# The first product of a mixture layer in seven block products instead of eight, with weight sums made on the chip

## The chip, the cores and the metric

The kernel runs on 1 core of one Trainium2 chip. The metric is the device time of one execution in microseconds, the median over the runs; before the change it is 940.54 us (3 runs, 940.5 to 940.66).

## The reference

Attention over a window of 128 keys with a bias that falls with distance, and behind it two matrix products with a squared Relu between them:

```python
def _attn_ref(q, k, v):                     # each (8, 8, 576, 64)
    scores = scale * np.matmul(q, k.transpose(0, 1, 3, 2))
    ...
    mask = (rel >= 0) & (rel < window)      # window = 128
    scores = np.where(mask, scores + bias[None], -1000000000.0)
    ...
    attn = attn / (np.sum(attn, axis=-1, keepdims=True) + 1e-09)
    return np.matmul(attn, v)

def _moe_ref(x, w_in, w_out):               # (4608, 512), (512, 2048), (2048, 512)
    h = np.maximum(x @ w_in, 0.0)
    return h * h @ w_out
```

x is the attention's output with the heads put side by side. All is float32.

## The kernel before

The 4608 tokens are cut into 9 chunks c of 512, and the 2048 hidden columns into 16 blocks f of 128. Everything is kept transposed: features on the partitions, tokens on the columns. Each float32 operand of the two large products is split into a high and a low part (type float32r), and a product is the sum of three: high by high, high by low, low by high.

**First product** (`gemm1`, L192; matmuls L200): for one chunk and one block f, four slices of 128 input features by three parts, 12 matmuls of 128x128 weights and 512 columns, into one bank `g` of the accumulation memory. Then a Relu on ScalarE (ACT, L210), the square on VectorE (DVE, L213), the high part on ACT (L217) and the low part on DVE (L219). **Second product** (`gemm2`, L221; matmuls L229): 12 matmuls more, four output blocks m by three parts, into four banks `acc` that collect over the 16 blocks f.

**Weights.** All 16 slots of an arena in the on-chip memory hold one block f of both matrices each (`weights_load`, L160). They come in as 64 bit floats and are converted on the chip (`convert`, L167) to a high and a low word that lie side by side, so the columns of a weight block are 8 bytes apart. In some blocks (`APART`, L39: first matrix, every fourth f, first two slices) neighbouring columns are dealt to two blocks, which makes the step 16 bytes. The weights stay on the chip to the end.

**Attention.** A `Couple` q is a pair of heads of a chunk; four make one chunk's x. A `visit` (L533) does, on the PE, the products of the old couple with its values (L541), in two phases, and between them the scores of the new couple (L548), which go into a pair of banks `big` (the same that `g` uses, one buffer) and into `s`. Then ACT and DVE take the scores out (`front`), `out` (L524) makes the x parts of the old couple (ACT high, DVE low), and `soft` and `squares` make the weights of the new couple: minimum on DVE, exponential on ACT (L257), normalisation on POOL (L269), a transpose on DVE (L321), four DMAs to DRAM (L325), one DMA back (L330), and two masks on POOL (L334). The second half of a couple is done in `rest`, whose exponentials are ordered behind the Relu of a first product. The next visit needs both halves.

**Order.** PE's order is written out by hand; the other engines are put in order by the compiler's scheduler, by priority and by its own estimate of time; blocks under `high_priority` go first. Chunk 0 and the first couples run under a planner (`Plan`, L632) with costs and due times in `start` (L683). From block n = 16 on a loop (L807) does the first product of block n and the second product of block n - 2 in turn, and every fourth n (`FIRST` = 39, counted in half steps) a visit between the two. All DMAs but a few go through the queue of SyncE (SP).

The accumulation memory is full: `s` two banks, `acc` four, `big` two.

Of the kernel before, what the change touches and what calls it, by code (L numbers as in the profile page):

```python
# [12 lines left out]
I32 = mybir.dt.int32  # L13
# [14 lines left out]
HEAT = 16  # L28
HOLD = lambda f: (('n', 3),) if f < 1 else (('n', 6),) if f < 2 else (('z', 7),)
# [8 lines left out]
FIRST = 39  # L38
# [23 lines left out]
class Kern:  # L62
    def __init__(self, ctx, tc, qkd, vd, w1d, w2d, cstd, outd):
        self.tc, self.nc = tc, tc.nc
        self.qkd, self.vd = qkd, vd
        self.w1d, self.w2d, self.cstd, self.outd = w1d, w2d, cstd, outd
# [9 lines left out]
        self.dr = ep("dr", 4, space=bass.MemoryType.DRAM)  # L76
        self.sc = ep("sc", 1, space=PSUM)
# [16 lines left out]
        self.start_banks = [self.ac.tile([128, 512], F32, name="acc") for _ in range(4)]  # L94

    def join(self, ctx):
        self.later.close()
        self.big = ctx.enter_context(self.tc.tile_pool(name="big", bufs=1, space=PSUM))
# [61 lines left out]
    def weights_load(self, f):  # L160
        nc = self.nc
        at = lambda name, dt: nc.alloc_sbuf_tensor_at(f"{name}{f}", [128, 2, 512, 2], dt, offset=self.arena + f * 8192).ap()
        self.raw[f], self.w[f] = at("raw", I32), at("w", F32R)
        for i, d in enumerate((self.w1d, self.w2d)):
            nc.sync.dma_start(self.raw[f][:, i].rearrange("p d t -> p (d t)"), d[f].bitcast(I32))
# [17 lines left out]
    def block(self, i, f, b):  # L183

        w = self.w[f][:, i]
# [34 lines left out]

    def gemm2(self, c, f):  # L221
        nc = self.nc
# [3 lines left out]
        for m in range(4):  # L226
# [5 lines left out]
            if f == NF - 1:  # L232
# [3 lines left out]
                (nc.scalar if c == NCH - 1 and m == 3 else nc.sync).dma_start(out, o)  # L236

# [135 lines left out]
class Couple:  # L373
# [150 lines left out]
    def out(self, S):  # L524
# [4 lines left out]
        self.K.nc.scalar.copy(halves(self.u[:, 0]), self.X)  # L529
        self.nc.vector.tensor_tensor(halves(self.u[:, 1]), self.X, halves(self.u[:, 0].bitcast(F32)), op=ALU.subtract)  # L530


def visit(K, old, new):  # L533
# [18 lines left out]
    for made in phase((1, 0), False)[:2]:  # L552
        K.tc.add_manual_dep(made.ins, turn.ins.name, SYNC, reason="halves of the keys change banks")
    if new:
        new.front()
    old.out(S)
# [126 lines left out]
def start(K):  # L683
# [91 lines left out]
    for f in range(NF + 2):  # L775
        if f < NF:
            g = K.gemm1(0, f)
            step, n = lambda g=g: next(g, None), len(CONVERT) - 1
            if f == 0:
                P.add("g1a", "PE", 2.1, tuple(last) + (("c", f, n),), GO, step, "g")  # L780
                last = ["g1a", ("l", 6), ("l", 7)]
            P.add(("g1", f), "PE", 2.8 if f else 0.7, tuple(last) + (("c", f, n),), 500 if f else GO, step, "g" if f else None)
# [6 lines left out]
        if 1 < f < NF:  # L789
            P.add(("g2", f - 2), "PE", 2.8, (("g1", f), ("h1", f - 2, 3)), 500, do(K.gemm2, 0, f - 2))  # L790
# [5 lines left out]
def tile_attn_moe(ctx: ExitStack, tc: tile.TileContext, *aps):  # L796
    K = Kern(ctx, tc, *aps)
    K.const()
    with tc.manual_schedule(engines={ENGINES["PE"]}):
# [7 lines left out]
        for n in range(NF, NF * NCH + 2):  # L807
            for t in (2 * n, 2 * n + 1):
                q, part = divmod(t - FIRST, 8)
                q += 9  # L810
                with tc.high_priority(offset=50):
                    if part == 0:
                        if q + 1 < 4 * NCH:
                            K.load(*divmod(q + 1, 4))
                        if q < 4 * NCH:
                            late = pairs[q] = Couple(K, q)
                        if q - 1 in pairs:
                            visit(K, pairs.pop(q - 1), late)
                        if late:
                            late.turn(0)  # L820
                if t % 2 == 0 and n < NF * NCH:
                    for _ in K.gemm1(*divmod(n, NF)):
                        pass
                    if late:
                        with tc.high_priority(offset=50):
                            late.rest()
                            late.turn(1)
                        late = None
                if t % 2:
                    K.gemm2(*divmod(n - 2, NF))  # L830
# [57 lines left out]
```

## Time and profile before

| | us |
|---|---|
| median of 3 runs | 940.54 |
| the profiled execution | 940.21 |
| its span | 938.5 |
| chunk 0 (36.8 to 137.7) | 100.9 |
| one chunk after it (137.7 to 238) | 100.3 |
| TensorE matmuls busy | 928.9 |
| VectorE, ScalarE, GpSimd busy | 501.5, 417.4, 210.2 |

The profile is of one execution. PE is TensorE's matmuls, PEld its weight loads, which run beside matmuls; DVE is VectorE, ACT ScalarE, POOL GpSimd, SP SyncE. A row of a group names line, engine, operation, out<-in, shapes and count, then busy time in us and the mean of one in ns, then the idle time of the engine before them and what ended it. A row of a timeline has the start in us, the length in us, the instructions and their count. Matmuls overlap in the pipeline, so the distance from start to start counts and not the recorded length.

### The profile page before, as it was taken

To read this page: it belongs to the slowest core of one execution; us is meant where nothing else is said; L and a number is where in the kernel's file an instruction comes from. 1 tells how busy PE (TensorE), PEld (TensorE's weight loads), DVE (VectorE), ACT (ScalarE), POOL (GpSimd) and SP (SyncE) were. 2 spreads that over 40 slices of the span, in tenths; PEclk is the share of its full clock that TensorE was granted. 3 is DMA by queue.
4 is the path that set the end of the run, shared out by engine and by line. 5 is a ranking of instruction groups with operands and counts; after the bars stand their busy time and mean duration, and the time that the engine had idled before them with its cause. 6 is when DMAs were issued, how large, how long until landed. Compare 5 with 4: busy or idle time off the path is not lost.

```text
span 938.5 us, 19487 instructions
## 1 busy us (share of the span) xinstructions
PE 928.9 (99%) x7488; PEld 782.9 (83%) x7492; DVE 501.5 (53%) x1334; ACT 417.4 (44%) x1107; POOL 210.2 (22%) x254
## 2 busy tenths in 40 slices
PE   8899999999999999999999999999999999999998
PEld 5688888888888888888888888888888888888886
DVE  6999874445554555545555454555455455433222
ACT  7898753343444444334434343334444444322222
POOL 4213331222221222222222222221222222220000
PEclk9999999999999999999999999999999999999999
DMA  9975424222433333232433232324322231111001
GB/s 341 404 287 167 136 73 130 72 62 82 130 86 85 83 99 108 63 86 80 124 85 86 77 105 77 86 85 121 94 76 83 75 92 43 38 46 45 1 0 45
DMA packets 72894, 95.26 MB, mean 101 GB/s; under 512 B 8033, under 2 KB 41953, under 8 KB 72801
## 3 DMA queue, kind: packets, MB, share of 16 engines
q1 hardware_dynamic: 72368, 93.36, 32.6%
q8 instruction: 59, 0.97, 0.4%
q10 hardware_dynamic: 432, 0.66, 0.3%
q14 instruction: 35, 0.28, 0.1%
HBM read 67.76 MB, written 26.21 MB: 100 GB/s over the span
## 4 chain that ended last, share of the span: by engine, by line
PE 95%; DMA 3%; DVE 1%; ACT 1%; issue 0%; POOLq 0%; DVEq 0%
PE acc L229 43%; PE g L200 42%; PE s L541 5%; PE g L548 2%; DMA raw<-in_dram 2%; PE s L548 1%; PE at L346 1%; DMA wide<-in_dram 1%; DMA qk<-in_dram 0%; ACT t L470 0%; PE s L412 0%; PE at L412 0%; DVE t L482 0%; DVE pp L625 0%; DVE tw L609 0%
## 5 line engine op out<-in xcount | busy, mean ns | idle before, releaser
L200 PE MATMUL g<-xu,w 128*128 128x512 f32 x1728 | 423.5, 394 | 1.4 <-issue 0.8
L200 PEld LDWEIGHTS g<-xu,w 128*128 128x128 f32 x1728 | 344.4, 209 | 56.8 <-issue 1.7
L229 PE MATMUL acc<-hh,w 128*128 128x512 f32 x1152 | 385.8, 396 | 0.0
L229 PEld LDWEIGHTS acc<-hh,w 128*128 128x128 f32 x1152 | 224.0, 194 | 45.7 <-issue 5.3
L210 ACT ACTIVATE r<-g 128x512 f32<-128x512 f32 x144 | 86.2, 599 | 352.4 <-PE g L200 352.2
L213 DVE TENSOR_TENSOR r<-r 128x512 f32<-128x512 f32 x129 | 92.4, 716 | 254.0 <-ACT r L210 254.0
L229 PE MATMUL acc<-hl,w 128*128 128x512 f32 x576 | 226.5, 393 | 0.0
L219 DVE TENSOR_TENSOR hl<-r,hh 128x512 fp32r<-128x512 f32 x144 | 122.0, 847 | 74.9 <-ACT hh L217 72.8
L334 POOL TENSOR_SCALAR_AFFINE_SELECT pp<-pp 128x512 f32<-128x512 f32 x128 | 109.8, 858 | 221.4 <-DMA pp<-way 173.5
L269 POOL TENSOR_TENSOR t<-t,nm 128x512 f32<-128x512 f32 x64 | 74.9, 1172 | 260.6 <-DVE nm L265 233.5
L229 PEld LDWEIGHTS acc<-hl,w 128*128 128x128 f32 x576 | 112.2, 195 | 19.6
L217 ACT CAST hh<-r 128x512 fp32r<-128x512 f32 x144 | 89.3, 620 | 78.2 <-DVE r L213 76.7
L257 ACT ACTIVATE t<-t,nm 128x128 f32<-128x128 f32 x256 | 100.1, 394 | 11.3 <-DVE nm L250 11.2
L321 DVE STREAM_TRANSPOSE pp<-t 128x512 f32<-128x512 f32 x64 | 45.1, 707 | 44.3 <-POOL t L269 38.6
L250 DVE CUSTOM_DVE_ANT_0 t<-t,cst 128x128 f32<-128x128 f32 x256 | 59.0, 295 | 1.0
L541 PE MATMUL s<-pp,v 64*64 64x128 f32 (+1 forms) x1792 | 52.0, 248 | 0.1
L541 PEld LDWEIGHTS s<-pp,v 64*64 64x64 f32 x1792 | 40.5, 134 | 10.1 <-issue 9.7
L257 ACT ACTIVATION_READ_ACCUMULATOR t<-t,nm 128x1 f32 x256 | 48.7, 190 | 0.0
L482 DVE COPY_PREDICATED t<-cst,s 64x256 f32<-64x256 int32 x100 | 44.5, 445 | 6.9 <-ACT t L463 3.8
L472 POOL MEMSET t<- 64x128 f32 (+1 forms) x44 | 10.0, 229 | 117.2 <-PE s L548 110.1
L529 ACT CAST xu<-s 128x512 fp32r<-128x512 f32 x28 | 16.4, 587 | 41.8 <-DVE t L482 26.9
L470 ACT COPY t<-g 64x256 f32<-64x256 f32 (+2 forms) x86 | 27.9, 340 | 3.7 <-PE g L548 1.0
(68 smaller groups left out, 480.5 us busy)
## 6 DMA issues: line engine op xcount, KB each, us to landing
raw<-in_dram SPq DMA_DIRECT2D x32, 512.0 KB, 8.7
way<-pp SPq DMA_DIRECT2D x256, 64.0 KB, 2.0
pp<-way SPq DMA_DIRECT2D x64, 256.0 KB, 2.7
qk<-in_dram SPq DMA_DIRECT2D x32, 320.0 KB, 3.1
v<-in_dram SPq DMA_DIRECT2D x32, 320.0 KB, 3.9
qk<-in_dram SPq DMA_DIRECT2D x38, 256.0 KB, 4.3
out_dram<-o SPq DMA_DIRECT2D x35, 256.0 KB, 2.6
v<-in_dram SPq DMA_DIRECT2D x3, 256.0 KB, 5.3
```

Of the source, the lines that this page charges most:

```text
L200: nc.tensor.matmul(g, w, xs[cc][:, part], start=i == 0, stop=i == 11)
L210: self.relu = nc.scalar.activation(r, g, AF.Relu)
L213: nc.vector.tensor_tensor(r, r, r, op=ALU.mult)
L217: nc.scalar.copy(hh, r)
L219: nc.vector.tensor_tensor(hl, r, hh.bitcast(F32), op=ALU.subtract)
L229: nc.tensor.matmul(self.acc[m], w, h, start=(f == 0 and i == 0), stop=(f == NF - 1 and i == 2))
L250: self.nc.vector.tensor_tensor_reduce(self.t[:, m], self.t[:, m], self.K.nrel(2 * self.p + m // 2), -0.125, BIG, ALU.add, ALU.min, self.nm ...
L257: return self.nc.scalar.activation(self.t[:, m], self.t[:, m], AF.Exp, bias=nm[:, 4 + m : 5 + m], scale=-1.0, accum_out=nm[:, m : m + 1],)
L269: self.nc.gpsimd.tensor_tensor(*(x.rearrange("p (j i) c -> p j i c", j=2) for x in (self.t, self.t)), self.rec.unsqueeze(3).to_broadcast([ ...
L321: nc.vector.transpose(squares.rearrange("p b m c -> p m b c"), self.t.rearrange("p m (b c) -> p m b c", c=32))
L334: nc.gpsimd.affine_select(to, self.own, pattern=[[-32 * sign, 4], [0, 4], [-sign, 32]], compare_op=op, fill=0.0, base=0, channel_multiplie ...
L541: made.append(mm(to, w, x, start=first and n < 2, stop=not first, skip_group_check=True))
```

## The change

In chunks 0 and 1 the first product stays as it was. From chunk 2 on (7 chunks) it is made for two blocks f at once (`seven`): the 512 input features, the 256 hidden columns and the 512 tokens are each halved, and the 2x2 block product is made of seven block products after Strassen and Winograd instead of eight. Each is 2 slices by 3 parts, 6 matmuls of 128x128 weights and 256 columns. The products are collected in two banks, which take the place of `big`: P in one, on which four products are summed one after the other, R and Q in the other. After each product ACT copies or DVE copies or adds the bank to a tile `four` of the on-chip memory; then Relu and square are one DVE instruction, and high and low part follow as before. Between the products stand the quarters of a second product (`second`), and a whole second product behind them.

Four of the seven weight operands are sums of weight blocks. `weight_sums` makes them once, in chunk 1, two pairs of blocks at each of the four visits there: seven operations on POOL, one on ACT, one on DVE, DMAs of all seven operands to DRAM (1.835 MB for a pair of blocks). `stream` brings the seven operands of a pair back in two DMAs into one of two buffers `flow`, for each of the 56 pairs. The buffers lie in the arena, in slots of first-matrix weights that are done with; for that the arena's 16 units now hold two blocks f of one matrix each (`UNITS`), loaded in the order in which they are first needed.

The four x operands that are sums are made in `out`: `tee` for the first two couples of a chunk (ACT 3, DVE 2, POOL 1 instructions of 256 columns in place of ACT 1 and DVE 1 of 512), `tees` for the last two (three more subtractions on DVE, three more copies on ACT, three subtractions on POOL). For the last couple of a chunk `out` goes ahead of `front`. `rest` now comes behind the first of the seven products, its exponentials behind the copy of P.

The diff, cut to its core:

```diff
+UNITS = [(0, 0)] + [x for p in range(NF // 2 - 1) for x in ((0, p + 1), (1, p))] + [(1, NF // 2 - 1)]
+UNIT = lambda i, f: UNITS.index((i, f // 2))
-FIRST = 39
+FIRST = 19
...
+    def weight_sums(self, j):
+        nc, sums = self.nc, self.sums[j]
...
+        for k, x in ((0, one), (3, words(w, 0)[:, 1]), (5, words(w, 1)[:, 1])):
+            nc.sync.dma_start(sums[:, k], x)
+        for m in range(2):
+            nc.gpsimd.tensor_tensor(lo[:, m], w[:, m, :, 0], w[:, m, :, 1], op=ALU.add)
...
+        nc.gpsimd.tensor_tensor(s1, a21, a22, op=ALU.add)
+        nc.gpsimd.tensor_tensor(as11(s2), as11(s1), a11, op=ALU.subtract)
+        nc.gpsimd.tensor_tensor(as11(s3), a11, as11(a21), op=ALU.subtract)
+        nc.gpsimd.tensor_tensor(s4, a12, s2, op=ALU.subtract)
+        nc.scalar.copy(lo.bitcast(F32R), hi)
+        nc.vector.tensor_tensor(hi.bitcast(F32R), hi, lo, op=ALU.subtract)
+        nc.sync.dma_start(sums[:, 1:3], words(both, 1))
+        nc.sync.dma_start(sums[:, 4:7:2], words(both, 0))
+
+    def stream(self, n):
+        if n >= NCH * NF // 2:
+            return
+        sums = self.sums[n % 8]
+        for i, x in enumerate(self.flow[n % 2]):
+            self.nc.sync.dma_start(x.bitcast(F32), sums[:, 4 * i : 4 * i + 4 - i])
...
+    def seven(self, n):
+        nc = self.nc
+        c, j = divmod(n, 8)
+        one, two = self.banks("one", "two")
+        P = one.tile([128, 512], F32, name="chain")[:, 0:256]
+        g = two.tile([128, 512], F32, name="rest")
+        R, Q = g[:, 0:256], g[:, 256:512]
+        four = self.four
+        def product(to, i, name, start=False):
+            todo = []
+            for (wh, wl), (xh, xl) in zip(self.operand(n, i), self.halves(c, name)):
+                todo += [(wh, xh), (wl, xh), (wh, xl)]
+            for k, (w, x) in enumerate(todo):
+                nc.tensor.matmul(to, w, x, start=start and k == 0, stop=k == 5, skip_group_check=True)
+        first = lambda: self.tc.high_priority(offset=600)
+        add = lambda to, x: nc.vector.tensor_tensor(to, to, x, op=ALU.add)
+        product(P, 0, "B11", True)
+        with first():
+            self.relu = nc.scalar.copy(four[:, 0, 0:256], P)
+        yield
+        product(R, 1, "T1", True)
+        with first():
+            nc.vector.tensor_copy(four[:, 1, 256:512], R)
+        product(P, 2, "T2")
+        with first():
+            nc.scalar.copy(four[:, 0, 256:512], P)
+        yield
+        product(Q, 3, "B21")
+        with first():
+            add(four[:, 0, 0:256], Q)
+        product(P, 4, "T3")
+        with first():
+            add(four[:, 1, 256:512], P)
+        yield
+        product(R, 6, "B22")
+        with first():
+            add(four[:, 0, 256:512], R)
+        product(P, 5, "T4")
+        with first():
+            nc.scalar.copy(four[:, 1, 0:256], P)
+        self.banks("big")
+        for f in range(2):
+            r = four[:, f]
...
+            nc.vector.scalar_tensor_tensor(r, r, 0.0, r, op0=ALU.max, op1=ALU.mult)
+            nc.scalar.copy(hh, r)
+            nc.vector.tensor_tensor(hl, r, hh.bitcast(F32), op=ALU.subtract)
...
+    def tees(self):
...
+        nc.scalar.copy(halves(self.u[:, 0]), self.X)
+        nc.vector.tensor_tensor(raws[0], x1, raw[:, 256:512], op=ALU.subtract)
+        nc.vector.tensor_tensor(raws[2], x0, raws[0], op=ALU.subtract)
+        nc.vector.tensor_tensor(raws[1], x1, raw[:, 0:256], op=ALU.subtract)
+        nc.vector.tensor_tensor(halves(self.u[:, 1]), self.X, halves(self.u[:, 0].bitcast(F32)), op=ALU.subtract)
+        for i in range(3):
+            nc.scalar.copy(hi[i], raws[i])
+            nc.gpsimd.tensor_tensor(lo[i], raws[i], hi[i].bitcast(F32), op=ALU.subtract)
...
+    if old.both[0].p == 3:
+        old.out(S)
     if new:
         new.front()
-    old.out(S)
+    if old.both[0].p < 3:
+        old.out(S)
...
+        for n in range(NF, 2 * NF):
+            for _ in K.gemm1(*divmod(n, NF)):
+                pass
...
+            if (n - FIRST) % 4 == 0 and n >= FIRST:
+                with tc.high_priority(offset=50):
+                    late = call(n)
+                for j in range(2):
+                    K.weight_sums((n - FIRST) // 2 + j)
+            K.gemm2(*divmod(n - 2, NF))
+            if n == 2 * NF - 4:
+                K.stream(NF)
+        K.stream(NF + 1)
+        for n in range(NF, NCH * NF // 2):
+            seconds = K.second(*divmod(2 * n - 2, NF))
+            for k, _ in enumerate(K.seven(n)):
+                if k == 0 and late:
+                    rest(late)
+                    late = None
+                if n % 2 and k == 1:
+                    K.stream(n + 1)
+                next(seconds)
+            for _ in seconds:
+                pass
+            if n % 2:
+                K.stream(n + 2)
+                with tc.high_priority(offset=50):
+                    late = call(2 * n + 1)
+            K.gemm2(*divmod(2 * n - 1, NF))
+        for n in range(NF * NCH - 2, NF * NCH):
+            K.gemm2(*divmod(n, NF))
```

`call` loads the next couple's inputs, does the visit and starts the first half's way through DRAM; `operand` takes the weight parts out of `flow`, 8 bytes apart, and `halves` the x parts.

140 lines of the change are left out of this document (104 added, 36 removed).

## The prediction

> **What bounds the kernel now.** I read the page's engine shares first, then the chain of waits, then stretches of one period, then the single matmuls.
>
> ```profile
> span 938.5 us, 19487 instructions
> PE 928.9 (99%) x7488; PEld 782.9 (83%) x7492; DVE 501.5 (53%) x1334; ACT 417.4 (44%) x1107; POOL 210.2 (22%) x254
> PE 95%; DMA 3%; DVE 1%; ACT 1%; issue 0%; POOLq 0%; DVEq 0%
> ```
>
> TensorE is busy for 99% of the span and holds 95% of the chain, so time is won only where PE does less, and lost where PE is made to wait. The views by stretch and the chain in order of time show the steady state:
>
> ```profile
> 0.00:36.80 36.80, 33.24 (x312) 21.25 (x316) 27.45 (x109) 28.21 (x85) 13.83 (x18) 1.00 0.97 364
> 36.80:137.70 100.90, 99.30 (x698) 83.03 (x697) 89.05 (x196) 81.01 (x179) 29.83 (x34) 1.00 0.58 195
> 408.50:433.57 25.07, 25.07 (x217) 21.40 (x216) 12.62 (x36) 9.78 (x28) 6.57 (x8) 1.00 0.27 79
> ...
> 411.62 3.00 PE acc L229 x12
> 436.69 2.98 PE acc L229 x12
> ```
>
> Columns of the first three: stretch, its length, busy PE, PEld, DVE, ACT, POOL, clock, DMA share, GB/s. The chain repeats every 436.69 - 411.62 = 25.07 us (one visit of an attention pair, and four blocks of each product), and in such a period PE is never idle, at the full clock (1.00). DVE has 12.6 of 25.1 us to do, ACT 9.8, POOL 6.6, and the DMA engines are 27% busy.
>
> What does one matmul of 512 columns cost? Its recorded duration (394 ns) overlaps the next; the pace is what counts. The timeline of PE:
>
> ```profile
> L200 PE MATMUL g<-xu,w 128*128 128x512 f32 x1728 | 423.5, 394 | 1.4 <-issue 0.8 <-DVE xu L530 0.6
> ...
> 500.67 2.92 PE L200 MATMUL g<-xu,w 128*128 128x512 f32 x12
> 503.43 0.39 PE L229 MATMUL acc<-hh,w 128*128 128x512 f32 x1
> ```
>
> Twelve matmuls in 503.43 - 500.67 = 2.76 us: 0.230 us each. A pair of blocks of the first product now takes 24 of them, 5.52 us.
>
> **The products.** For 56 pairs of blocks (7 chunks by 8) the 24 matmuls of 512 columns become 7 products of 6 matmuls of 256 columns: 42. If the pace simply halves (0.115), that is 4.83 us; but each still needs its own load of 128x128 weights, which no longer hides behind 512 columns. How fast can loads follow each other? Three kinds of rows bear on it (groups by form, and timelines):
>
> ```profile
> L229 PEld LDWEIGHTS acc<-hh,w 128*128 128x128 f32 x1152 | 224.0, 194 | 45.7 <-issue 5.3
> ...
> L200 PEld LDWEIGHTS g<-xu,w 128*128 128x128 f32 x5 | 1.2, 310 | 0.0
> 188.07 1.34 PE L200 MATMUL g<-xu,w 128*128 128x512 f32 x5
> ...
> L581 PEld LDWEIGHTS s<-qk__202 64*128 64x128 f32 x8 | 0.5, 186 | 0.2 <-DVE pp L625 0.2
> 17.33 0.52 PEld L581 LDWEIGHTS s<-qk__202 64*128 64x128 f32 x8 [0.17 <-DVE pp L625]
> ```
>
> The ordinary load (columns 8 bytes apart, high and low parts interleaved) is recorded at 194 ns. The loads of the blocks kept apart (columns 16 bytes apart) are recorded at 310 ns, yet their matmuls follow at (1.34 - 0.40)/4 = 0.235 us: a next one starts 75 ns before the recorded end. At L581 (4 bytes apart) eight loads go in pairs, one to each half of the rows, recorded at 186 ns; four pairs fit in 0.52 us, so a pair follows after (0.52 - 0.19)/3 = 0.11, again 75 ns before the end. Two rows with the same overlap: I take 194 - 75 = 119 ns for the ordinary load, just above the 115 ns of the columns, and so a pace of **0.120 us**. The streamed sums keep the 8 byte step. Ends: 0.115 (columns alone) and 0.230 (no overlap: today's pace, in which a load of 194 ns stands alone); near the two rows 0.115 to 0.130 is likely.
>
> Sum: 56 x (24 x 0.230 - 42 x 0.120) = 56 x (5.52 - 5.04) = 26.9 us. The blocks kept apart go too: 7 chunks x 4 blocks x 6 matmuls x 0.005 = 0.8. Together **-27.7 us**.
>
> The Trainium skill, TensorE: Matmul & The Clock Gate, section "LDWEIGHTS (loading the stationary operand)", says that a load takes its columns divided by 1.2 ns, whatever the matmul's width, which speaks against narrow matmuls: seven products want 42 loads for 24. By its figure 107 ns the load would still just fit; the rows here give 119 ns for this step, so it just doesn't.
>
> **The hand-overs inside a pair.** Five times a product goes into a bank that ACT or DVE must first have read: P after each of its copies or adds, the shared bank of R and Q after the copy of R and after the add of Q. Between lie always a quarter of a second product (3 x 0.23) and one other product (6 x 0.12): 1.41 us. How soon is such a bank read?
>
> ```profile
> 420.01 2.92 PE L200 MATMUL g<-xu,w 128*128 128x512 f32 x12
> 422.97 0.60 ACT L210 ACTIVATE r<-g 128x512 f32<-128x512 f32 x1 [2.87 <-PE g L200]
> ...
> L470 ACT COPY t<-g 128x256 f32<-128x256 f32 x1 | 0.4, 373 | 0.0
> L482 DVE COPY_PREDICATED t<-cst,s 64x256 f32<-64x256 int32 x12 | 5.3, 444 | 0.7 <-ACT t L463 0.6
> L217 ACT CAST hh<-r 128x512 fp32r<-128x512 f32 x16 | 9.9, 620 | 8.7 <-DVE r L213 8.6
> L219 DVE TENSOR_TENSOR hl<-r,hh 128x512 fp32r<-128x512 f32 x16 | 14.3, 895 | 8.5 <-ACT hh L217 8.3
> L530 DVE TENSOR_TENSOR xu<-s,xu 128x512 fp32r<-128x512 f32 x4 | 2.8, 692 | 0.1
> ```
>
> The last matmul's end is 422.93, the Relu starts 0.04 later; the next matmul could start at 422.77, so reading begins 0.20 after that. ACT needs 0.37 for 256 columns, DVE between 0.35 (half of 692) and 0.44: done after 0.57 to 0.64, with some 0.1 to tell PE 0.7. That leaves 0.7 us for an instruction in the way: ACT's longest is 0.62 (hidden), DVE's 0.90 (0.2 late at worst). Ends: nothing, and 3 hand-overs of DVE x 0.2 x 56 = 34 us if each met the longest. DVE spends about a seventh of its time in that one (14.3 of 100 us), and is seldom caught at its beginning: I take **+2 us**. DVE's load per period becomes 12.6 + 8 x 0.37 + up to 1.1 for new operands = 16.7 of 24, ACT's about 10.7, POOL's 8.6: none becomes a bound by its sum.
>
> **The visits.** A visit needs the two halves of the previous pair, written to DRAM and read back, then cut by POOL. The period shrinks by 2 x 0.48 to 24.1 us. Is the chain short enough? Timelines of PE, SP and POOL from one visit:
>
> ```profile
> 408.82 0.90 PE L541 MATMUL s<-pp,v 64*64 64x64 f32 x32
> ...
> 418.75 1.77 SPq L325 DMA_DIRECT2D way<-pp  x4
> 421.90 0.34 SPq L330 DMA_DIRECT2D pp<-way  x1
> 422.50 1.74 SPq L325 DMA_DIRECT2D way<-pp  x4
> 425.92 0.34 SPq L330 DMA_DIRECT2D pp<-way  x1
> ...
> 428.80 1.84 POOL L334 TENSOR_SCALAR_AFFINE_SELECT pp<-pp 128x512 f32<-128x512 f32 x2 [2.12 <-DMA pp<-way]
> ```
>
> From 408.82 to 430.64: 21.8 us; of 25.07 that leaves 3.2 us, of 24.1 it leaves 2.3. Into this chain come: three more 256-column copies on ACT and three subtractions on DVE for a late pair (1.1 us each; 0.5 on ACT for an early one), the handing over of P, R and Q (one or two 0.4 us pieces in front of something), and the streams on the same queue. Out of it goes some of the wait of the second half's exponentials, since they now follow the first copy of a pair of blocks and not a whole first product (2.76 - 0.72 = 2 us of PE time, of which about 1 us counts, as the first half's exponentials end only then). Two streams of 7 x 512 x 4 x 128 = 1.835 MB per period move 3.67 MB; the loading stage moved 364 GB/s at 97% share, so 375 GB/s at 100%, and they need 9.8 us of the DMA engines in 24: their share goes from 0.27 to about 0.7. A write or read of the chain then stands behind a stream for some part of 1 MB, 2.8 us. I put the additions at 0.9 to 3 us against 2.3 us left, a mean overrun of 0.25 us, x 24 visits that fall in these chunks: **+6 us**. Ends: 0 (all within the slack) and 24 x 2.5 = 60.
>
> **Costed at nothing.** One row for POOL:
>
> ```profile
> L269 POOL TENSOR_TENSOR t<-t,nm 128x512 f32<-128x512 f32 x64 | 74.9, 1172 | 260.6 <-DVE nm L265 233.5
> ```
>
> Weights in units of one matrix and two blocks: a first block 2p now needs 2p slots loaded instead of 2p + 1, and chunk 0 had 100.90 - 99.30 = 1.6 us of idle PE to win; if the planner's order turns out worse, one conversion chain of a few us. The weight sums in chunk 1: two operations of 512 columns and four of 256 per pair of blocks, 4 x 1.17 = 4.7 us of POOL, 9.4 per visit (a copy more in every second pair), beside 6.6 of 25 us: POOL's free time hides them; without it, the normalisation waits behind one of them (1 us, four visits, and 3 us of slack). The streams themselves: each slot is refilled when its pair is done, and used 10 us later; 4.9 us of transfer fit. At a chunk's start the products with B11 and T1 come first, so the last pair's new operands have two products and two quarters more; if that isn't enough, 1 us x 7.
>
> **The sum.** -27.7 + 2 + 6 = -19.7. The profiled run took 940.2 (its span 938.5), so 920.5; the median of the shown runs is 0.3 higher: **920.8 us**.
>
> **Rivals.** (1) Slower: the streams hold up the visits. A stream's 1 MB half is issued when its slot comes free, and SP issues in order; if it lies in front of the second half's writes or of its read at every visit, the chain is 21.8 + 0.9 + 2.8 = 25.5, with 0.2 for PE's start 25.7, against 25.07 now: 24 x 0.6 = +15, less 4 for the last chunk, which has no visits: 952; with a whole stream (4.9 us) in front about 1000. It decides from 25.3 us of chain on. For it: 2.3 us of slack only, one queue; against: most of a period has no burst. 20%. (2) The hand-overs: if DVE is late by 0.15 us at each of its three, 56 x 3 x 0.15 = 25 us more, 944: the gain is gone. 10%. (3) No overlap of loads, pace 0.230: 56 x 42 x 0.11 = +259 on the forecast, near 1180. Both rows with other steps speak against it: 3%. (4) Better: pace 0.115 and no waits: 56 x 0.69 + 0.8 = 39, 901 us. 10%. The Trainium skill's section "Back-to-back issue gap" of the same page gives columns/2.4 + 2.5 ns, 109 ns for 256; by that the estimate would be 887, but for 512 it gives 216 where the trace has 230.
>
> That fewer products are made than the change says can't be: the count is in the loop, 56 x 42.
>
> **How the numbers follow.** The forecast has 57%, its own range 911 to 931 (pace 0.117 to 0.124, waits 2 to 15). The range of 903 to 950 takes in most of (4) and (2) and about half of (1). 0.2%, about 1.9 us, is what a measurement of this kernel can tell from no change: faster than that is the forecast, (4) and a third of (2), 0.70; within it some of (2), 0.04; slower the rest, 0.26.
>
> **What would show it.** Right: 2352 matmuls of 256 columns at 0.12 us, the 128x512 first product down to 384 matmuls, the period at 24.1 to 24.4 us. Wrong: a pace above 0.13; PE idle before L541-like lines released by POOL's cut or by a DMA (1); PE idle inside pairs released by DVE (2).

## The result, and the profile after

| | before | after |
|---|---|---|
| median, us (4 runs each) | 940.6 (940.5 to 940.66) | 1006.63 (1004.76 to 1008.53) |
| ratio | | 1.0704, 95% interval 1.069 to 1.0717 |
| the profiled execution, its span | 940.21, 938.5 | 1004.76, 1003.1 |

The kernel became 7% slower; 920.8 was forecast. The page of the kernel after: the span, the engines' shares, the chain, two of the costliest groups, the DMA issues (what goes where, queue, count, KB of each, median us from issue to landing).

```profile
span 1003.1 us, 22438 instructions
PE 936.0 (93%) x8496; PEld 817.7 (82%) x8500; DVE 602.3 (60%) x1622; ACT 435.1 (43%) x1241; POOL 290.8 (29%) x362
PE 52%; DMA 17%; DVE 12%; POOL 8%; ACT 6%; issue 3%; SPq 1%; POOLq 0%; DVEq 0%; ACTq 0%
...
L309 PE MATMUL rest<-xu,flow 128*128 128x256 f32 x1008 | 150.7, 286 | 9.3 <-DVE four L319 5.6
...
L222 PE MATMUL g<-xu,w 128*128 128x512 f32 x384 | 98.9, 407 | 11.2 <-ACT r L232 11.2
...
flow<-ws SPq DMA_DIRECT2D x56, 1024.0 KB, 5.4
flow<-ws SPq DMA_DIRECT2D x56, 768.0 KB, 5.3
...
way<-pp SPq DMA_DIRECT2D x256, 64.0 KB, 3.2
pp<-way SPq DMA_DIRECT2D x64, 256.0 KB, 3.7
```

Before, the chain that ended last was PE for 95%; now it is PE for 52%, and DMA, DVE, POOL and ACT hold 43%. So PE's work alone no longer sets the time: nearly half of the chain is work of others for which PE waits. The same halves of a couple go through DRAM as before, but more slowly; the page of before has

```profile
way<-pp SPq DMA_DIRECT2D x256, 64.0 KB, 2.0
pp<-way SPq DMA_DIRECT2D x64, 256.0 KB, 2.7
```

**Where the time went.** The starts of the first visit, of the fifth and of the last, in the timeline of PE, before and after:

```profile
157.37 0.46 PE L541 MATMUL s<-pp,v 64*64 64x64 f32 x12
...
258.46 0.56 PE L541 MATMUL s<-pp,v 64*64 64x64 f32 x16
...
835.87 0.57 PE L541 MATMUL s<-pp,v 64*64 64x64 f32 x16
```

```profile
160.89 0.57 PE L702 MATMUL s<-pp,v 64*64 64x64 f32 x16
...
294.97 0.34 PE L702 MATMUL s<-pp,v 64*64 64x64 f32 x8 [2.51 <-POOL pp L465]
...
903.44 0.32 PE L702 MATMUL s<-pp,v 64*64 64x64 f32 x2
```

| stretch | before | after | difference |
|---|---|---|---|
| up to the first visit | 157.4 | 160.9 | +3.5 |
| four periods: the weight sums are made (chunk 1) | 101.1 | 134.1 | **+33.0** |
| 23 periods: seven products (chunk 2 on) | 577.4 | 608.5 | **+31.1** |
| from the last visit to the end | 102.6 | 99.7 | -2.9 |

Only the tail, which has no visits, got shorter. In the 23 periods the forecast took a period without waits as 24.1 us, so 23 x 24.1 = 554; the measured 608.5 hold 54 us of loss. These two numbers, 33 and 54, are what the experiments have to explain. What the 33 are made of can be read at once: from 160.9 to 295.0 PE is busy for 109.7 of 134.1 us, so 24.4 are idle time, and the granted clock of 0.94 there costs up to 8 more.

The waits of PE in the kernel after (line, releaser: us in total, times, longest):

```profile
PE s L702 <- POOL pp L465: 21.0, 20, 5.0
PE chain L309 <- ACT four L315: 12.3, 13, 2.7
PE g L222 <- ACT r L232: 11.2, 5, 3.5
PE rest L309 <- DVE four L319: 5.6, 4, 2.9
```

L465 is POOL's mask, the last link of a half's way through DRAM; L319 DVE's copy of R; L315 ACT's first copy of P; L232 the Relu of the old first product, which remains in chunks 0 and 1.

And the stretches (columns as in the prediction), of chunk 1 before, then after, and of 100 us of the steady part after:

```profile
137.70:238.00 100.30, 100.30 (x870) 85.60 (x869) 47.94 (x126) 37.50 (x100) 22.59 (x30) 1.00 0.30 85
```

```profile
137.70:238.00 100.30, 88.38 (x700) 74.26 (x697) 49.83 (x104) 37.84 (x93) 62.92 (x64) 0.97 0.49 157
238.00:340.00 102.00, 88.23 (x786) 77.24 (x785) 59.17 (x167) 42.34 (x134) 36.82 (x46) 0.93 0.62 204
...
550.00:650.00 100.00, 94.73 (x979) 84.88 (x978) 60.45 (x178) 41.16 (x130) 26.18 (x35) 0.98 0.70 229
```

No engine is full: in chunk 1 POOL has 63 of 100 us and PE still stands idle for 12. The eighth column, the granted clock, was 1.00 throughout before; now it is 0.93 to 0.98. The timeline of PE shows what that is:

```profile
591.60 0.88 PE L309 MATMUL chain<-xu,flow 128*128 128x256 f32 x6
592.32 0.40 PE L359 MATMUL acc<-hh,w 128*128 128x512 f32 x1
...
592.79 0.39 PE L359 MATMUL acc<-hh,w 128*128 128x512 f32 x1
593.02 0.88 PE L309 MATMUL rest<-xu,flow 128*128 128x256 f32 x6
596.56 1.04 PE L309 MATMUL chain<-tees,flow 128*128 128x256 f32 x6 [2.66 <-ACT four L315]
597.40 0.63 PE L359 MATMUL acc<-hh,w 128*128 128x512 f32 x1
597.83 0.63 PE L359 MATMUL acc<-hl,w 128*128 128x512 f32 x1
598.25 0.63 PE L359 MATMUL acc<-hh,w 128*128 128x512 f32 x1
598.68 1.48 PE L309 MATMUL rest<-xu,flow 128*128 128x256 f32 x6
```

Up to 593.02 all is as forecast: six products of 256 columns in 592.32 - 591.60 = 0.72 us, 0.120 each. Then PE stands for 2.66 us, and behind that the 512-column matmuls start 0.42 to 0.43 us apart and not 0.23, and six of 256 columns last 1.28 (the step from 598.68 to the next product at 599.96) and not 0.72. So a wait can cost a slow stretch behind it besides its own length. In this trace every stretch at half clock lasts 3.41 us (this one starts at 597.37; the last one is cut off by the end), and all start whole multiples of 3.41 us apart. Each follows a slice of that grid in which PE stood for 1.83 us or more in all, and of the other slices behind the loading of weights (from 37 us on) none has more than 1.88: the idle time within one slice counts, not the length of a single wait. The Trainium skill, TensorE: Matmul & The Clock Gate, section "What's actually happening", gives half clock after an idle window of about 3.4 us; its 1.2 GHz make 427 ns of 512 columns, which the 0.42 to 0.43 here agree with; but here 2.60 of the 2.66 us fell into one such window and were enough, so it needn't be idle throughout.

Who made PE stand? The timeline of ACT at that place:

```profile
593.99 0.40 ACT L388 ACTIVATE t<-t,nm 128x128 f32<-128x128 f32 x1 [1.91 <-DVE nm L381]
...
595.77 0.39 ACT L388 ACTIVATE t<-t,nm 128x128 f32<-128x128 f32 x1
596.07 0.19 ACT L388 ACTIVATION_READ_ACCUMULATOR t<-t,nm 128x1 f32 x1
596.16 0.35 ACT L315 COPY four<-chain 128x256 f32<-128x256 f32 x1
```

P was complete at 591.60 + 0.88 = 592.48. ACT was idle then, but its next instruction in program order was an exponential that waited for DVE's minimum until 593.99; four of them stand before the copy, which so began 3.7 us after P was complete.

### The profile page after: what moved, and what is told of

Read it like the earlier page. It is cut to its first block, busy times and chain, and to the rows that moved or that the text cites. A ratio compares the mean times of both kernels' runs of the same rounds, so it can differ in the third digit from the quotient of the medians.

```text
span 1003.1 us, 22438 instructions
## 1 busy us (share of the span) xinstructions
PE 936.0 (93%) x8496; PEld 817.7 (82%) x8500; DVE 602.3 (60%) x1622; ACT 435.1 (43%) x1241; POOL 290.8 (29%) x362
## 4 chain that ended last, share of the span: by engine, by line
PE 52%; DMA 17%; DVE 12%; POOL 8%; ACT 6%; issue 3%; SPq 1%; POOLq 0%; DVEq 0%; ACTq 0%
PE acc L359 22%; PE chain L309 10%; PE rest L309 8%; DMA pp<-way 5%; PE g L222 4%; POOL pp L465 4%; DMA way<-pp 3%; DMA flow<-ws 3%; PE s L702 3%; DVE t L381 3%; DVE t L613 3%; DMA raw<-in_dram 2%; PE g L709 2%; ACT t L601 2%; ACT t L388 2%
## 5 line engine op out<-in xcount | busy, mean ns | idle before, releaser
L465 POOL TENSOR_SCALAR_AFFINE_SELECT pp<-pp 128x512 f32<-128x512 f32 x128 | 104.0, 820 | 306.3 <-DMA pp<-way 196.0
L309 PEld LDWEIGHTS rest<-xu,flow 128*128 128x128 f32 x1008 | 147.6, 198 | 24.0 <-DVE four L319 10.0
L309 PE MATMUL chain<-tees,flow 128*128 128x256 f32 x1008 | 152.4, 287 | 13.6 <-ACT four L315 12.3
L309 PE MATMUL rest<-xu,flow 128*128 128x256 f32 x1008 | 150.7, 286 | 9.3 <-DVE four L319 5.6
L309 PEld LDWEIGHTS chain<-tees,flow 128*128 128x128 f32 x1008 | 134.7, 199 | 18.1 <-ACT four L315 15.6
L222 PE MATMUL g<-xu,w 128*128 128x512 f32 x384 | 98.9, 407 | 11.2 <-ACT r L232 11.2
L400 POOL TENSOR_TENSOR t<-t,nm 128x512 f32<-128x512 f32 x64 | 68.0, 1066 | 142.5 <-DVE nm L396 139.5
L222 PEld LDWEIGHTS g<-xu,w 128*128 128x128 f32 x384 | 78.0, 214 | 26.7 <-ACT r L232 13.3
L343 DVE SCALAR_TENSOR_TENSOR four<-four 128x512 f32<-128x512 f32 x112 | 81.7, 766 | 2.5 <-ACT four L336 0.4
L345 DVE TENSOR_TENSOR hl<-four,hh 128x512 fp32r<-128x512 f32 x112 | 77.2, 718 | 6.7
L702 PE MATMUL s<-pp,v 64*64 64x64 f32 (+1 forms) x1792 | 61.1, 261 | 21.1 <-POOL pp L465 21.0
L344 ACT CAST hh<-four 128x512 fp32r<-128x512 f32 x112 | 68.8, 620 | 23.0 <-DVE four L343 22.6
L319 DVE COPY four<-rest 128x256 f32<-128x256 f32 x56 | 23.4, 418 | 87.1 <-PE rest L309 86.8
```

Source lines behind the costliest of these rows:

```text
L222: nc.tensor.matmul(g, w, xs[cc][:, part], start=i == 0, stop=i == 11)
L309: nc.tensor.matmul(to, w, x, start=start and k == 0, stop=k == 5, skip_group_check=True)
L343: nc.vector.scalar_tensor_tensor(r, r, 0.0, r, op0=ALU.max, op1=ALU.mult)
L344: nc.scalar.copy(hh, r)
L345: nc.vector.tensor_tensor(hl, r, hh.bitcast(F32), op=ALU.subtract)
L400: self.nc.gpsimd.tensor_tensor(*(x.rearrange("p (j i) c -> p j i c", j=2) for x in (self.t, self.t)), self.rec.unsqueeze(3).to_broadcast([ ...
```

## The experiments

Each time is one run; the four runs of the kernel after lie 3.8 us apart, so a difference of less than 4 us isn't read. "Four" and "23" are the two stretches of the table above (134.1 and 608.5 in the kernel after). Line numbers of an experiment are its own. The kernel before took 940.2 to 940.6 beside them.

### The weight sums in chunk 1

**e5_no_sums**: all arithmetic of `weight_sums` goes, its DMAs stay in the program and write other data.

> Leaves out the arithmetic of the weight sums in chunk 1: the seven operands sent to DRAM are plain weight blocks, so the result is another. DMAs stay. If the arithmetic on POOL, ACT and DVE is what makes the first four periods 134 us in place of 101, they fall to 101 to 106 and the time to 972 to 980 us. If the 14.7 MB of writes or the seven products at its end do it, they stay over 120 and the time over 990.

992.74 us. Four: 101.7, as good as before's 101.1. But the DMAs didn't keep their place: all 40 of them are issued between 48.9 and 130.1 us, where in the kernel after 20 of the 40 are issued between 170.4 and 274.0, beside the four periods. So this run takes away the arithmetic and the DMAs beside it, and doesn't tell which of the two made the 33 us; e14 below does, in part. (The total fell by 12 only: a wait of 12.2 us, `PE s L523 <- DVE t L597`, appeared ahead of the first visit, which came at 173.4, and the 23 took 616.2, 8 more. I put the wait down to the earlier place of the DMAs, which wasn't tried.)

How can so little arithmetic cost that much? The timeline of ACT, then of POOL, in chunk 1 of the kernel after:

```profile
181.36 1.09 ACT L268 CAST both<-both 128x1024 fp32r<-128x1024 f32 x1 [4.26 <-POOL both L267]
182.35 0.59 ACT L232 ACTIVATE r<-g 128x512 f32<-128x512 f32 x1
```

```profile
178.07 1.45 POOL L265 TENSOR_TENSOR both<-both 128x256 f32<-128x256 f32 x1
179.48 1.04 POOL L400 TENSOR_TENSOR t<-t,nm 128x512 f32<-128x512 f32 x1
180.49 0.84 POOL L267 TENSOR_TENSOR both<-both 128x256 f32<-128x256 f32 x1
182.47 2.93 POOL L465 TENSOR_SCALAR_AFFINE_SELECT pp<-pp 128x512 f32<-128x512 f32 x2 [1.15 <-DMA pp<-way]
```

ACT idles for 4.26 us at its one cast of the sums, since POOL isn't done with them; the Relu that PE needs stands behind it. And POOL's own normalisation (L400), a link of the visit, stands between the sums.

**e2_sums_late**: the last ACT and DVE steps of the sums two blocks later in the program.

```diff
         nc.gpsimd.tensor_tensor(s4, a12, s2, op=ALU.subtract)
+        yield
         nc.scalar.copy(lo.bitcast(F32R), hi)
...
+            if made and (n - FIRST) % 4 == 2:
+                for x in made:
+                    next(x, None)
```

> The last two steps of the weight sums (ACT's copy and DVE's subtraction, with their DMAs) are put two blocks later in the program, the POOL steps stay. Theory A expects chunk 1 to lose its waits for the Relu (11 us, and some 4 of slow clock behind them), since ACT no longer stands in front of POOL's result: 980 to 992 us, periods of the first four visits near 27. Rival C (POOL's own added work delays normalisation and masks in chunk 1) expects at most 5 us: over 1000.

1005.78 us, four 132.4: no difference. ACT's order came out the same, for the scheduler places the cast by its own estimate of time. So this run tells nothing about the cause.

**e8_cast_behind**: the same, with the order forced.

```diff
+        cast = nc.scalar.copy(lo.bitcast(F32R), hi)
+        self.tc.add_manual_dep(cast.ins, self.relu.ins.name, ORDER, reason="sums of weights behind the Relu")
```

> As in the run with the last two steps of the weight sums put later, which left ACT's order as it was; here ACT's copy is tied behind the Relu of two blocks later, so that it stands behind it in ACT's order. Theory A expects the waits for the Relu in chunk 1 (11 us) and most of the added length of the first four periods to go: 980 to 992 us. Rival C (POOL's work is what delays) expects over 1000.

1003.54 us, four 128.3. The waits of PE:

```profile
PE s L704 <- POOL pp L467: 29.6, 17, 10.1
...
PE g L222 <- ACT r L232: 3.3, 3, 1.7
```

The wait for the Relu fell from 11.2 to 3.3 us, so the cast did hold it; but the wait for the masks rose from 21.0 to 29.6, with 10.1 in one piece at the fifth visit. PE was held up on two sides at once: freeing ACT alone brought 6 us in the stretch and nothing in all.

**e10_sums_dve**: the sums' additions on DVE in place of POOL.

```diff
-            nc.gpsimd.tensor_tensor(lo[:, m], w[:, m, :, 0], w[:, m, :, 1], op=ALU.add)
+            nc.vector.tensor_tensor(lo[:, m], w[:, m, :, 0], w[:, m, :, 1], op=ALU.add)
...
-        nc.gpsimd.tensor_tensor(s1, a21, a22, op=ALU.add)
+        nc.vector.tensor_tensor(s1, a21, a22, op=ALU.add)
```

> The weight sums' additions and subtractions on DVE in place of POOL. Rival C (POOL's work in chunk 1 delays normalisation and masks, and ACT waits for it) expects the first four periods to fall from 134 us to 105 to 112 and the time to 978 to 985. If any added work in these two queues does it, whichever engine, they stay over 125: over 995.

1004.05 us, within the spread in all; four 126.9, 7 us less. POOL has its time back, yet the wait for the Relu is 12.4 us, the longest 5.1. The timeline of ACT there:

```profile
179.61 1.10 ACT L268 CAST both<-both 128x1024 fp32r<-128x1024 f32 x1 [4.22 <-DVE both L267]
```

ACT's cast still stands ahead of the Relu and still waits over 4 us, now for DVE. So taking the load off POOL isn't enough.

**e14_sums_placed**: every step gets a place. Additions of even pairs on POOL behind the second normalisation, of odd pairs on DVE behind the second transpose, the cast behind the Relu of a later block.

```diff
+        eng, after = (nc.gpsimd, self.normed) if j % 2 == 0 else (nc.vector, self.turned)
+        put = lambda x: self.tc.add_manual_dep(x.ins, after.ins.name, ORDER, reason="sums of weights behind the half")
...
+            put(eng.tensor_tensor(lo[:, m], w[:, m, :, 0], w[:, m, :, 1], op=ALU.add))
```

> All is computed; the weight sums of even pairs stay on POOL, tied behind the second half's normalisation, those of odd pairs go to DVE, tied behind its transpose, ACT's copy behind the Relu of a later block. If the sums' place in the queues costs the 33 us of chunk 1, the first four periods fall from 134 to 105 to 112 us and the time to 975 to 985. If their amount does, they stay over 125 and the time over 995.

995.06 us; four 116.0, the periods 25.1, 26.5, 27.6 and 36.8. Of 33 us 18 are back with the same arithmetic, and with 20 of the 40 DMAs issued between 167.8 and 280.2, seven of them in the period of 26.5 us. So these 18 are neither the amount of arithmetic nor the DMAs beside it; what changed is where the sums stand in the queues. But three things changed at once: half of the additions went to DVE, where they are shorter, the additions got a place, and the cast got one. The runs nearest to the parts, e10 and e8, brought 7 and 6 us in this stretch; the place of the additions alone wasn't tried. The stretch lies between the two ranges expected, the total at the edge of the second. (The total fell by 10, since the first visit came 1.9 us later, the 23 took 1.2 and the tail 5.3 more.) The fourth period, in which the last sums meet the first seven products, stays long.

### The streams

**e1_no_streams**: the later streams are left out (`if n >= NF + 2: return`), the products use old weights.

> Leaves out the streams of all pairs but the first two, so that later pairs are multiplied with the wrong weights. Theory A (fixed order: ACT and DVE work in order, and a hand-over stands behind an instruction that itself waits) expects little of the streams: 998 to 1005 us, PE still waiting for the first copy of P (12 us before) and for the masks. Rival B (the streams hold up SP and the DMA engines, and so the halves' way through DRAM) expects PE's wait for POOL's masks (24 us in this profile) to go nearly whole: 975 to 985 us.

988.87 us; 23: 593.7. The streams cost some 16 us; the time lies between the two ranges expected, for PE's wait for the masks fell from 21.0 to 13.7 us and didn't go.

**e9_small_streams**: a quarter of each stream's columns; as many DMAs, with the same waits.

```diff
+            a = 512 if n < NF + 2 else 128
+            self.nc.sync.dma_start(x.bitcast(F32)[:, :, 0:a], sums[:, 4 * i : 4 * i + 4 - i, 0:a])
```

> The streams bring a quarter of the columns (later pairs are multiplied with partly wrong weights); their number, their waits and their place in SP's queue stay. Leaving the streams out had given 16 us. If the DMA engines' load did that, most of the 16 us comes here too: 988 to 993 us. If SP's order did it (a stream waits for PE, and the halves' writes stand behind it), it doesn't: 1000 to 1006.

988.38 us; 23: 595.4. As much comes back as without the streams, so the cost is the bytes in the DMA engines; nothing beyond the spread is left for SP's issues and waits.

**e13_streams_behind**: all bytes, but each stream ordered on SP behind the current couple's read back from DRAM.

```diff
+            if n > NF + 1:
+                self.tc.add_manual_dep(d.ins, self.read.ins.name, ORDER, reason="streams behind the halves")
```

> All is computed; only SP's order is changed: each stream is tied behind the DMA that reads the current couple's second half back, so that its bytes move when no half is on its way. If the 16 us come from streams and halves moving at the same time, most of them come back: 988 to 995 us, the read landing 21 to 22 us after the visit's start in place of 24.5. If it is the amount of bytes, or if the later streams come too late for PE, 1003 or more.

987.09 us; 23: 593.7, as without streams. PE's wait for the masks fell from 21.0 to 10.0 us. The page's DMA issues:

```profile
flow<-ws SPq DMA_DIRECT2D x56, 1024.0 KB, 6.4
flow<-ws SPq DMA_DIRECT2D x56, 768.0 KB, 6.6
...
way<-pp SPq DMA_DIRECT2D x256, 64.0 KB, 1.8
pp<-way SPq DMA_DIRECT2D x64, 256.0 KB, 2.8
```

Writes and reads of the halves are back at 1.8 and 2.8 us (2.0 and 2.7 before, 3.2 and 3.7 after), and the streams, which nobody waits for that closely, take 6.4 in place of 5.4. It was a collision in time, not an amount.

### The hand-overs and x's sums

**e7_no_adds**: DVE's four reads of the banks (copy of R, three adds) are left out.

> Leaves out DVE's four hand-overs of a pair (the copy of R and three additions), so the result is another; ACT's three copies stay. If DVE, held by its hand-overs, delays the attention chain, the waits for masks and the periods fall by 0.5 to 1 us: 975 to 990 us. If ACT alone couples the two chains, it stays within 5 us of 1005.

1001.41 us, 23: 605.6. With none of DVE's hand-overs the time stays within the spread: they aren't what holds PE. The wait for ACT's first copy is longer than the 12.3 us before, `PE chain L311 <- ACT four L317: 18.7, 18, 3.2`, so part of what DVE cost may have gone over to ACT.

**e3_soft_late**: the first half's exponentials ordered behind the first copy of P (`late.both[0].soft(K.relu)` moves into the call of `rest`).

> In the chunks with seven products the first half's exponentials are ordered behind the first copy of P, as the second half's are. Theory A expects PE's wait for that copy (L315, 12 us and the slow clock behind it) to go: 985 to 995 us. Rival D (the attention chain is too long by its own added work) expects the wait to move to POOL's masks and no gain: 1000 to 1010.

1002.57 us, 23: 608.5. Waits of PE:

```profile
PE chain L309 <- ACT four L322: 16.5, 20, 1.2
...
PE chain L309 <- ACT four L315: 3.1, 5, 1.2
```

The first copy (L315) is free, 12.3 to 3.1, and the second one (L322) is held in its place, 1.0 to 16.5. The time is in the range of the rival, but its reason, more waiting for the masks, isn't the main one: that wait is 23.4 us, 2.4 more. The exponentials and the copies share ACT at the same time, and one goes first.

**e6_no_tees**: the sums of x (`tee`, `tees`) aren't made, other halves are used for them.

> Leaves out the sums on the x side: the operands are made as before the change (one copy on ACT, one subtraction on DVE), and the products take plain x parts, so the result is another. Theory D (the attention chain is too long by its added work) expects the steady periods (25.3 to 28 us) to fall by 1 us or more each: 970 to 985 us. Theory A without D (hand-overs stand behind waiting instructions) expects under 0.5 us each: 993 to 1003.

987.86 us, 23: 594.7: x's sums cost 14 to 17 us, which lies between the two ranges expected. They stand on DVE and ACT ahead of the minima and the copies; how much of the cost comes from each engine wasn't tried.

**e4_out_after**: one part undone: the last couple's x behind the scores again, as before the change.

```diff
-    if old.both[0].p == 3:
-        old.out(S)
     if new:
         new.front()
-    if old.both[0].p < 3:
-        old.out(S)
+    old.out(S)
```

> For the last couple of a chunk the x operands are made behind the new couple's front again, as for the other three. Theory A expects the periods that begin with such a visit (27 to 29 us against 25 to 26 of others) to shorten by about 2 us, 7 times: 990 to 997 us. If the new operands are then needed too early (the products with T2 and B21 wait for them), it is slower: over 1010.

996.08 us, 23: 598.2. This part of the change lost 9 to 10 us by itself. The first product of the next chunk now waits for its new operands (`PE chain L309 <- ACT tees L690: 4.6, 4, 1.2`), which is less.

**e12_dve_out**: e10 and e4 together.

> Two mends together, everything is computed: the weight sums on DVE, and the last couple's x operands behind the front. If the two effects add up, 969 to 978 us.

997.5 us, four 130.3, 23: 602.0: no better than e4 alone, so the two effects don't add up.

### What is left without the additions, and the parts together

**e11_bare**: no streams, no sums of x, no DVE hand-overs.

> Leaves out the later streams, the sums on the x side and DVE's four hand-overs together (another result); the 42 products a pair, ACT's copies and the weight sums stay. If these three and the weight sums are all that eats the gain, the steady periods come to 24.1 to 24.5 us: 960 to 970. If they stay near 25.5, something of the seven products themselves (ACT's copies behind the exponentials) remains: over 980.

969.39 us; 23: 574.9, most periods 24.2 to 24.9, on average 25.0. So 34 of the 54 us are gone, and 21 are left against the forecast's 554. Of these PE's idle time is 10 (`PE chain L310 <- ACT four L316: 9.1, 12, 2.0` is most of it); the other 11 are work of PE: it is busy for 564.8 us.

**e15_three**: e13, e14 and e4 together. **e16_four**: and e3 besides.

> Streams behind the halves, sums placed, and the last couple's x operands behind the front, all computed. If the three effects add up (-13, -25, -9), 950 to 965 us.

> As the run before, and the first half's exponentials behind the first copy of P. If PE's wait for that copy is what remains (9 to 13 us and the slow clock behind it), it is 8 to 15 us less than the run before; if the second copy takes its place, as it did alone, the same within 3 us.

979.88 and 978.88 us. The gains of the three (18, 10 and 9, against 1004.76) don't add up: 25 in place of 36. In the 23 periods e15 with 599.1 is even behind e13 alone with 593.7; why is open. e3 again does nothing; e16 has `PE chain L315 <- ACT four L328: 18.0, 21, 1.2`.

**e17_spread**: e15, with more time between a copy and the product that needs the bank. For an even pair the eight quarters of both second products go between the seven products; before, the four of one.

```diff
             nc.vector.tensor_copy(four[:, 1, 256:512], R)
+        yield
         product(P, 2, "T2")
...
-            seconds = K.second(*divmod(2 * n - 2, NF))
+            quarters = [x for f in range(2 * n - 2, 2 * n - n % 2) for x in [K.second(*divmod(f, NF))] * 4]
+            seconds = lambda: next(quarters.pop(0), None)
```

> As the kernel with three edits together (streams behind the read, sums placed, x operands behind the scores; 979.88 us), and besides, for the first pair of blocks of each two the quarters of two second products, not of one, are spread between the seven products, so that PE has about 2.1 us instead of 1.41 us between the reading of a bank and the next product into it. All is computed, nothing is added. Theory A (the waits for the copies of P, and the slow clock behind them, come from the short slack of 1.41 us): the waits at L315 and L322 fall by more than half, 8 to 15 us less than with the three edits, 965 to 972 us. Theory B (what remains is the chain of the visit, or the second pair, in which nothing is changed): within 3 us of 980 us.

967.17 us, 13 less than e15; 23: 583.5 (e15 599.1). Waits of PE for the first copy of P in e15, then in e17:

```profile
PE chain L315 <- ACT four L321: 12.8, 17, 2.3
```

```profile
PE chain L315 <- ACT four L321: 3.9, 8, 0.8
```

The wait itself fell by 8.9 us, and the longest from 2.3 to 0.8. The granted clock, 0.98 in four of the five stretches of 100 us or so between 340 and 850 in e15, is 0.98 in one and 1.00 in four in e17. In the 23 periods e15 has four stretches at half clock and e17 one: 3 x 3.41 us at half clock are 5 us, which with the 8.9 make most of the 15.6 gained there. So the short slack is what made a held copy a wait, and the slow clock came with it.

No version beats the kernel before. What e17 still lacks against it, 27 us: 5 up to the first visit, 19 in the four periods with sums (29.2 and 39.8 for the last two), 6 in the 23, and 3 back in the tail. Why the last periods with sums stay long is not settled, nor the 5 us of chunk 0.

## Why the prediction was wrong

**The products (-27.7): the pace was right, but no run shows the whole saving.** The pace was 0.120 us, as worked out from loads of 194 - 75 ns (the loads of these products are recorded at 196 to 199), and rivals (3) and (4) fell with that. Yet in the 23 periods PE is busy for 577.4 us before, for 564.8 in e11 and for 567.4 in e17, where the forecast needs 554. About 5 of the missing us are the second products, taken as unchanged: their matmuls start 0.238 us apart on average in e11 and 0.233 before. The rest stays open.

**The weight sums in chunk 1, "costed at nothing": this step failed first, by 33 us.** I wrote that POOL's free time hides them, and priced the case without cover at "1 us, four visits". Two things were wrong. The size: a sum of 256 columns took 0.85 to 1.29 us of POOL where half of 1172 ns was assumed, and all additions together 53 us, not 38:

```profile
L264 POOL TENSOR_TENSOR both<-both 128x256 f32<-128x256 f32 x8 | 10.3, 1293 | 1.0 <-PE s L709 0.5 <-POOL both L258 0.3
...
L267 POOL TENSOR_TENSOR both<-both 128x256 f32<-128x256 f32 x8 | 6.8, 849 | 0.0
...
L268 ACT CAST both<-both 128x1024 fp32r<-128x1024 f32 x8 | 9.1, 1131 | 26.0 <-POOL both L267 26.0
```

But even so POOL is busy for 63 of 100 us. What decided is the last row: ACT stood idle for 26.0 us in eight casts. I had checked which engine has free time; I should have asked what is queued behind each new instruction that itself waits. e5 shows how much goes without the sums, e8 and e10 that moving one engine's share brings 6 or 7 and moves the wait, e14 that another place, with half of the additions on DVE, gives 18 of 33 back. Why the other 15 stay is open.

**The visits (+6): too small, by about 10 us for the streams and as much again for x's sums.** The chain of 21.8 us was read from one visit, and nearly the shortest: from a visit's start to the end of its last mask the median of the 23 periods is 22.4 us before, so 1.7 us were left in a period of 24.1 and not 2.3. After the change it is 26.0, above the rival's limit of 25.3 in 16 of the 23. It is 22.6 in e13, and 24.8 in e6, which leaves out x's sums; these, priced within the +6, cost 14 to 17 us. Rival (1) named the mechanism, halves behind streams, with a chance of 20%; I weighed one read or write behind a part of 1 MB. What happened is broader: each write lands 1.2 us later and each read 1.0 us later, and the streams' share of the loss (e1, e9, e13) is 16 us, about what the rival priced (15). The rival's condition was met, its time was not, since the other losses came on top. The rule that bears on it is in the Trainium skill, DMA: Bandwidth & Descriptors, section "Latency and other measured facts": access to DRAM takes 0.2 us on average and 2 us at high load, and the fixed cost of a DMA goes with it. 2.0 us at a DMA share of about 0.3 and 3.2 at 0.62 to 0.70 agree in kind; e13 shows that it is the load at that moment which counts, with 1.8 us at a share of 0.69 over the same 100 us.

**The hand-overs (+2): wrong in what holds them.** The slack of 1.41 us was worked out rightly, and DVE, on which I put the cost, wasn't the main part (e7). I took the longest single instruction in front of a copy, 0.62 us on ACT, as the worst that can be. An instruction that waits itself is no longer bounded by its length: four exponentials, the first of them behind minima on DVE, put the first copy 3.7 us behind P. e3 and e16 moved this wait to the next copy; e17, with more slack, took 13 us out. And each such wait was costed at its length only: with the granted clock at 0.97, 0.93 and 0.98 over the three kinds of stretches, 0.03 x 100 + 0.07 x 102 + 0.02 x 510 = 20 us are lost at most to slow matmuls behind waits, which the prediction hadn't as a term at all.

**The chunk's start, "two products and two quarters more" (7 us if short):** the cover for the new operands was nearly enough, but the price was paid at the other end: putting them ahead of the taking out of the scores cost 9 to 10 us (e4).

**The rest.** No chance went to several losses together of 33, 16, 14 and 10 us; the range took the forecast's waits as one case and each rival by itself, and ended at 950.

## What to carry to other kernels

When PE is at 99% and the kernel is held together by a fixed order on every engine, free time of an engine is no cover: for each added instruction ask what it waits for and what is queued behind it, on all engines that it passes. Give the places of new work by hand, just behind the last link of the critical chain (e13 got 18 us back, and e14, which also moved half of the additions to DVE, 18 of 33 in its stretch, with the same work). And a saving in PE's time shortens the very intervals in which the others were hidden, so weigh how much slack is left between a bank's reading and its next use before counting the saving.

## What the runs showed of the hardware

- Matmuls of 256 columns with a load each follow each other at 0.120 us, though the loads are recorded at 196 to 199 ns: successive loads overlap by some 75 ns, in this form too.
- Half clock came in slices of 3.41 us on a fixed grid, behind a slice in which PE stood for about half. Over the traces of all nineteen kernels, from 37 us on, every slice with more than 1.93 us of idle time had half clock behind it, and no slice at full clock with less than 1.44. That is why waits of nearly the same length differ: twelve matmuls of 512 columns behind 2.41 us took 3.07 us, behind 2.47 us 4.39 (the timeline of PE in chunk 1). Of the 2.41 us 1.88 fell into one slice, of the 2.47 us 2.05:

```profile
174.65 3.07 PE L222 MATMUL g<-xu,w 128*128 128x512 f32 x12 [2.41 <-ACT r L232]
...
183.00 4.39 PE L222 MATMUL g<-xu,w 128*128 128x512 f32 x12 [2.47 <-ACT r L232]
```

- The same 256-column additions of the weight sums took, on average by line, 0.42 to 0.57 us on DVE and 0.92 to 1.44 us on POOL (e14, which has both).
